# A fused long-convolution and MLP block on one core: the front's small rows turned on TensorE, two swap buffers exchanged, the half block of w3 on two column groups, and some sixty moves in a written order

## The chip, the cores and the metric

The kernel runs on one core of a Trainium2 chip. The time is that of one execution on the device, in microseconds (us). Engines: PE is TensorE (matrix multiplication), DVE VectorE, ACT ScalarE, POOL GpSimd, SP the engine whose queue issues most DMAs. PEld is PE's loading of weights, which overlaps its matmuls.

## The reference, cut to what matters

S = 2048 tokens, D = 640 channels, hidden width F = 1728, all in bf16.

```python
mod = silu(c) @ w_mod                      # six vectors: sa, ca, ga, sb, cb, gb
x = A_q
h = layernorm(x) * (1 + ca) + sa           # q of block A
k_shift[s] = sum over t<4 of k[s-t] * shift_k[:, t]
kv = k_shift * v
y = irfft(rfft(kv, 4096) * rfft(ssm_k, 4096))[:2048] + kv * ssm_D
x = x + ga * (h * y)
h = layernorm(x) * (1 + cb) + sb           # input of block B
g = gelu(layernorm(h) @ w1)                # its four channel quarters are shifted by 1, -1, 2, -2 tokens
x1 = h + shifted(g) @ w2
h2 = gelu(layernorm(x1) @ w3) @ w4         # w3: 640 x 1728, w4: 1728 x 640
return x + gb * (x1 + h2)
```

## The kernel before

The whole kernel is one list of tasks. `add(engine, cost, f, r=, w=)` of a `Planner` records a task: a function that emits instructions for one engine, and the keys (a buffer and a range of it) that it reads and writes. From the keys follow the dependences and thus the semaphores. The costs in `add` set nothing here: a string `ORDER`, written out in the source, gives the order in which the tasks are emitted and the engine of each (`88P:0` is task 88 on PE with PSUM place 0; S is SP, D DVE, A ACT, G POOL). Each engine runs its own tasks strictly in that order, and SP's order is the order of its DMAs. A task that waits holds back all that stands behind it on its engine.

Big buffers in SBUF are used again and again by range: `Ra`, `Rb`, `RG`, `RH`, `RK`, `RQ`, `R3`, `R5`, `T01`.

**Front (0 to about 20 us).** The long convolution is a Fourier transform of length 4096 in two stages of small matrix products. Its sine and cosine tables are made on the chip: POOL's iota gives integers, DVE scales them and masks them (`angles`, L292 and L293) or POOL does it in turns (`angles_pool`, L306 to L310), and ACT takes the sine (`sin_to` L321, `turns_to` L316). `F1bd` is the table of stage 1, `Gs` that of stage 2 (its third part is the negative of its first, L348). The per-partition constants for this (`pidx`, `pci`, `s32`, `s64`, `offc`) are 15 tiny DVE operations, L263 to L279. Meanwhile SP loads, in this order: D (L224, into `Dcol`, one column per block of 128 channels), four blocks of ssm_k (L228), shift_k (L229, into `skT`), the fifth block, then k and v by transposing DMAs (L233, `kT` and `vT`), and much later c (`c_col`, at 38.8 us). D and c come as 640 separate elements of 2 bytes, shift_k as 640 pieces of 8 bytes. D is added to the first tap of ssm_k (L444, three times on POOL, twice on DVE), and a block is turned in 32x32 squares by DVE (`to_slots`, L394).

**Transforms (8 to 95 us).** Stage 1 (L407) multiplies the turned blocks, first of ssm_k, then of kv, by `F1bd` into PSUM; ACT and DVE copy the result to `T01` (L207 is that copy on ACT, L209 on DVE). Stage 2 (L427) uses two row groups of 64 rows side by side. The shifts of k are matmuls with diagonal matrices (L463; `diagw`, made by POOL from `skT`, L355), and DVE multiplies by v (L468). The spectra are then multiplied (L617, DVE; 20 products). For these the upper and the lower halves of the partitions have to be swapped by pairs of DMAs (L613, one by SP, one by POOL) into a ring of four buffers:

```python
KSY = [(RG[:, 6144:8192], ...), (RK[:, 0:2048], ...), (RK[:, 2048:4096], ...), (Rb[:, 8192:10240], ...)]
```

The inverse goes through L628 and L629 and then, per group of token tiles, through 32x32 products (`inverse2`, L661).

**Modulation.** silu(c) is computed on POOL; PE multiplies it with w_mod, loaded in ten pieces (`mod_half`, L487, L493), and ACT writes the vectors (L497 to L508).

**Token tiles (56 to 299 us).** 16 tiles of 128 tokens go through `make_q` (first layer norm, L601, L602), `chain_a` (times q, L737, added to x, L740), `chain_b` (second layer norm, L755, L756), `chain_c` (third one, into the mixer). Layer norms take a sum from DVE, a sum of squares from ACT (`square_sum`, L729), a few tiny operations on POOL or DVE (`ln_finish`, L702 to L717), and a normalisation on DVE (L594) or ACT (L592). The normalised tile is turned by five PE matmuls (L772) and copied by ACT (L778) or DVE (L780), or it is turned by SP's transposing DMA (L765). Then PE does w1 (L818, L828), w2 (L873; DVE adds, L880), and, in groups of one or two tiles with all tokens of a group side by side, w3 (`mm_w3`, L907) and w4 (`mm_w4`, L937). There are nine such groups: seven of two tiles, and two of one tile (the first and the last).

F = 1728 is 13 blocks of 128 and a **half block** of 64. Before, the half block of w3 is filled up to 128 columns with a second copy of its 64 columns (POOL, L1020), so that its matmuls are of the same shape as all others, and its result stands twice, on partitions 0 to 63 and 64 to 127. In w4 the half block multiplies 64 rows only: `half`, L928, takes tile 0 from the lower 64 partitions and tile 1 from the upper ones, on two row groups. ACT's gelu (L911) takes up to four blocks at a time, and the last piece holds blocks 12 and 13. DVE adds the rest (L960, L965, L966) and SP stores the tile in four DMAs (L969; for the last tile L981, L984, L987).

The main loops of `mm_w3` before:

```python
for fl in range(fn):
    fb = f0 + fl
    for b in range(ND):
        nc.tensor.matmul(pt[:, fl, 0:cw], lhsT=w3_sb[:, b, fb * P:(fb + 1) * P], rhs=xT[:, b, 0:cw],
                         start=(b == 0), stop=(b == ND - 1))
```

## Time and profile before

| | |
|---|---|
| time, median of 3 runs | 302.58 us (300.95 to 302.81) |
| span of the profiled execution | 298.7 us |
| what lies around the span, from span to median | 3.9 us |
| PE, DVE, ACT, POOL busy | 269.7, 218.2, 208.3, 104.8 us |
| mean granted clock of PE | 0.975 |
| first transpose, first matmul | 6.01, 8.12 us |
| PE busy of 40 us, 100 to 140 us | 29.6 us |
| last matmul starts | 293.69 us |

The profiled execution is known by its span alone, so its own time is taken as the span and the 3.9 us around it. The profile is that of one execution. Its rows give, for a group of instructions, the line of the source, the engine, the operation, out<-in with the shape, the count, the busy time and mean duration of one, and the idle time of the engine ahead of them with what ended it. Rows of the timeline give start and duration in us. Rows of the table by stage give the stretch and its length, the busy time and number of instructions of PE, PEld, DVE, ACT and POOL, the granted clock of PE (1 is full), the share of time for which the 16 DMA engines are busy, and GB/s. Matmuls are pipelined, and their ends are modelled, so a matmul's price is better read from the distance between starts.

### The profile page before, as it was taken

Reading aid. Unit: us, or ns where it says so; the run is one execution under the profiler, and the core shown is the slowest. Engines: PE = TensorE matmul, PEld = TensorE weight load, DVE = VectorE, ACT = ScalarE, POOL = GpSimd, SP = SyncE. Lnnn points to the kernel's source line nnn. Section 1 sums busy time; section 2 is a strip of 40 time slices with the busy share of each in tenths; the row PEclk is TensorE's granted clock in tenths of the full one; section 3 lists DMA queues with packets and bytes.
Section 4 is the critical chain, followed back from the end, with each engine's and each line's share of the span. In section 5 each row is a group of like instructions: output and inputs, shape, how many; then the busy total and the mean of one; then the engine's idle time right before and its main releaser. Section 6 shows DMA issues by size and latency. Waiting matters only on the chain.

```text
span 298.7 us, 7890 instructions
## 1 busy us (share of the span) xinstructions
PE 269.7 (90%) x3176; PEld 208.5 (70%) x3182; DVE 218.2 (73%) x438; ACT 208.3 (70%) x341; POOL 104.8 (35%) x237
## 2 busy tenths in 40 slices
PE   0999999999989766869999999999999999999993
PEld 0666755777878436648878677787788767887871
DVE  8998999999999998898759589886361544212442
ACT  4799989999999789979868775766854705431200
POOL 5864364453216591434275426120421321100000
PEclk9999999999999859799999999999999999999999
DMA  6999999898999920563700203223113030510112
GB/s 215 275 215 184 225 137 246 225 217 221 229 253 281 280 65 2 153 203 69 273 4 0 46 5 68 56 46 60 41 40 80 5 89 6 63 43 23 29 52 60
DMA packets 58356, 35.76 MB, mean 120 GB/s; under 512 B 40032, under 2 KB 55008, under 8 KB 58320
## 3 DMA queue, kind: packets, MB, share of 16 engines
q1 hardware_dynamic: 57136, 32.01, 46.3%
q0 software_dynamic: 1088, 3.21, 4.1%
q8 instruction: 25, 0.41, 0.6%
q14 instruction: 11, 0.09, 0.1%
q10 hardware_dynamic: 96, 0.04, 0.1%
HBM read 16.31 MB, written 2.62 MB: 63 GB/s over the span
## 4 chain that ended last, share of the span: by engine, by line
PE 51%; DVE 13%; ACT 11%; DMA 10%; POOL 6%; issue 5%; SPq 2%; DVEq 0%; POOLq 0%; ACTq 0%
PE ps_w L937 17%; PE ps_w L907 14%; ACT T L207 5%; DMA Ra<-in_A_q_dram 5%; PE ps_w L873 4%; PE ps_w L818 3%; PE ps_s L427 3%; ACT RG L729 3%; DVE Rb L617 3%; PE ps_ksh L463 2%; POOL lnv L715 2%; PE ps_s L407 2%; DMA RK<-R 2%; DVE R L756 2%; PE ps_mod L493 2%
## 5 line engine op out<-in xcount | busy, mean ns | idle before, releaser
L907 PE MATMUL ps_w<-R,T 128*128 128x256 bf16 (+1 forms) x630 | 63.8, 261 | 0.7 <-DMA R<-RH 0.7
L907 PEld LDWEIGHTS <-T 128*128 128x128 bf16 x630 | 55.5, 98 | 7.9 <-issue 2.0
L937 PE MATMUL ps_w<-T,R 128*128 128x320 bf16 x416 | 59.1, 299 | 0.0
L911 ACT ACTIVATE R<-ps_w 128x1024 bf16<-128x1024 f32 (+2 forms) x36 | 28.8, 827 | 41.9 <-PE ps_w L907 41.9
L937 PEld LDWEIGHTS <-R 128*128 128x128 bf16 x416 | 40.5, 98 | 15.2
L960 DVE TENSOR_TENSOR T<-ps_w,R 128x640 bf16<-128x640 f32 x15 | 12.3, 822 | 35.4 <-PE ps_w L928 18.1
L207 ACT CAST T<-ps_s 128x1024 bf16<-128x1024 f32 x32 | 30.4, 1029 | 3.2 <-PE ps_s L407 3.1
L207 ACT CAST R<-ps_s 128x960 bf16<-128x960 f32 (+1 forms) x35 | 30.8, 964 | 1.8 <-PE ps_s L427 1.6
L407 PE MATMUL ps_s<-F1bd,Rb 128*128 128x256 bf16 x160 | 23.3, 298 | 8.7 <-DVE Rb L394 8.1
L729 ACT ACTIVATE RG<-R 128x640 bf16<-128x640 bf16 x32 | 23.5, 734 | 9.9 <-DVE R L880 6.7
L407 PEld LDWEIGHTS <-Rb 128*128 128x128 bf16 x160 | 16.7, 107 | 14.7 <-DVE Rb L394 8.6
L873 PE MATMUL ps_w<-RG,R 128*128 128x320 bf16 x160 | 23.2, 299 | 2.1 <-ACT R L820 2.1
L715 POOL TENSOR_TENSOR lnv<-lnv,mhalf 128x2 f32<-128x2 f32 (+1 forms) x29 | 22.5, 775 | 2.3
L427 PE MATMUL ps_s<-T,RG 64*128 64x160 bf16 x512 | 21.2, 230 | 0.8 <-ACT R L207 0.6
L880 DVE SCALAR_TENSOR_TENSOR R<-ps_w,R 128x640 bf16<-128x640 f32 x16 | 12.9, 819 | 11.8 <-PE ps_w L873 11.6
L427 PEld LDWEIGHTS <-RG 64*128 64x128 bf16 x512 | 17.7, 94 | 5.1 <-issue 4.6
L818 PE MATMUL ps_w<-R,RG 128*128 128x256 bf16 (+1 forms) x200 | 20.0, 259 | 1.3 <-DMA R<-RK 0.6
L873 PEld LDWEIGHTS <-R 128*128 128x128 bf16 x160 | 15.4, 98 | 8.2 <-ACT R L820 2.4
L629 PE MATMUL ps_i<-EB,Rb 128*128 128x128 bf16 x160 | 19.0, 219 | 1.5 <-DVE Rb L617 1.4
L818 PEld LDWEIGHTS <-RG 128*128 128x128 bf16 x200 | 17.1, 102 | 3.5 <-issue 2.0
L628 PE MATMUL ps_i<-EA,Rb 128*128 128x128 bf16 x160 | 19.0, 219 | 0.4 <-ACT R L207 0.3
L714 POOL TENSOR_TENSOR lnv<-stat,lnv 128x2 f32<-128x2 f32 x19 | 4.0, 212 | 40.9 <-ACT RG L729 28.7
(178 smaller groups left out, 513.5 us busy)
## 6 DMA issues: line engine op xcount, KB each, us to landing
Ra<-in_A_ssm_k_dram SPq DMA_DIRECT2D x5, 512.0 KB, 5.7
R<-in_w_mod_dram SPq DMA_DIRECT2D x6, 400.0 KB, 6.0
out_dram<-RH SPq DMA_DIRECT2D x60, 40.0 KB, 1.6
T<-in_B_w_dram SPq DMA_DIRECT2D x5, 432.0 KB, 6.2
RH<-in_w_mod_dram SPq DMA_DIRECT2D x4, 400.0 KB, 4.4
Ra<-in_A_q_dram SPq DMA_DIRECT2D x4, 320.0 KB, 6.6
RK<-R SPq DMA_DIRECT2D x5, 256.0 KB, 4.5
RK<-R POOLq DMA_DIRECT2D x5, 256.0 KB, 5.3
```

The costliest lines, as they stand in the source:

```text
L207: nc.scalar.copy(dst, src(ps.tile))
L407: nc.tensor.matmul(psv[:, ml, :], lhsT=xL[:, s0:s0 + P], rhs=F1r, start=True, stop=True)
L427: nc.tensor.matmul(psv[:, g, j], lhsT=Gs[p, k, 64 - 64 * cc:192 - 64 * cc], rhs=T1h[h][p, cc * 32 + k], start=(cc == 0), stop=(cc == 1), t ...
L628: nc.tensor.matmul(psv[:, w, :], lhsT=Av[:, r_, :, g_], rhs=EAf, start=True, stop=False)
L629: nc.tensor.matmul(psv[:, w, :], lhsT=Bv[:, r_, :, g_], rhs=EBf, start=False, stop=True)
L715: nc.gpsimd.tensor_tensor(rs, rs, mhalf[:, 0:n], ALU.pow)
L729: add("ACT", 0.74, lambda e: nc.scalar.activation(junk, src, ACT.Square, scale=float(D) ** -0.5, accum_out=stat[:, li, 1, t:t + 1]), r=[sk ...
L818: nc.tensor.matmul(pt[:, fb, 0:cw], lhsT=w1_sb[:, b, 160 * fb:160 * fb + P], rhs=hT[:, b, 0:cw], start=(b == 0), stop=(b == ND - 1))
L873: nc.tensor.matmul(pt[:, hf, 0:320], lhsT=gsf[:, fb, c0:c0 + P], rhs=w2_sb[:, fb, 320 * hf:320 * hf + 320], start=(fb == 0), stop=(fb == 4))
L907: nc.tensor.matmul(pt[:, fl, 0:cw], lhsT=w3_sb[:, b, fb * P:(fb + 1) * P], rhs=xT[:, b, 0:cw], start=(b == 0), stop=(b == ND - 1))
L911: nc.scalar.activation(g3[g % 2][:, f0:f0 + fn, 0:cw], ps.tile[:, 0:fn, 0:cw], ACT.Gelu_apprx_tanh)
L937: nc.tensor.matmul(bank(i, hf), lhsT=gg[:, fb, i * P:(i + 1) * P], rhs=w4_sb[:, fb, 320 * hf:320 * hf + 320], start=(fb == 0 and i == 0), ...
```

## The change

It has four parts.

1. **Front.** D, shift_k and c are loaded as five contiguous rows each (128, 512 and 128 elements a row) into a free corner of `T01`; D first of all, the other two after three blocks of ssm_k. PE turns them with matmuls of five columns against a 5x5 identity (`eye`, made on POOL), one ahead of its first stage-1 matmul and five after two stage-1 tasks; ACT copies the result from PSUM (`Dcol`; `csk`, which holds c and shift_k). c is no longer loaded at 38.8 us. Of the tiny constants, DVE keeps 9 operations and POOL takes 6. The two 512-wide scale steps of the first table go from DVE to ACT (Identity), the negated table goes from DVE to ACT, two additions of D go from POOL to DVE. ACT's first instruction is a sine of one column.
2. **Swap buffers.** The third and fourth buffers of `KSY` are exchanged. The DMAs that write them change places on SP and POOL.
3. **Half block.** The copy that filled w3 up is gone. Its 64 columns are multiplied on two column groups: tile 0 into the lower 64 partitions, tile 1 into the upper 64 (in a group of one tile, that tile into both). So there are ten matmuls of 128 columns in place of five of 256 (or five of 128). Gelu's last piece is 384 columns wide in place of 512.
4. **Order.** Behind the front, some sixty tasks change place or engine. On PE the moves are by one to five places. From DVE to ACT go one evacuation of stage 1 (at 55 us) and six normalisations; from ACT to DVE three normalisations, two copies of turned tiles, one evacuation of the inverse and one of the modulation; from POOL to DVE three small statistics steps, and one back. On SP, a half load of w4 goes ahead of loads of w3, and stores of output tiles change order. PE has 233 tasks where it had 231, ACT 254 for 248, DVE 304 for 301, POOL 94 for 97, SP 169 as before.

The diff, without the string `ORDER`:

```diff
-    KSY = [(RG[:, 6144:8192], ("RG", 6144, 8192)), (RK[:, 0:2048], ("RK", 0, 2048)), (RK[:, 2048:4096], ("RK", 2048, 4096)), (Rb[:, 8192:10240], ("Rb", 8192, 10240))]
+    KSY = [(RG[:, 6144:8192], ("RG", 6144, 8192)), (RK[:, 0:2048], ("RK", 0, 2048)), (Rb[:, 8192:10240], ("Rb", 8192, 10240)), (RK[:, 2048:4096], ("RK", 2048, 4096))]
...
-    dma("SP", 8, lambda q: ld_tiny(q, Dcol[:], A_ssm_D.rearrange("(b p) -> p b", p=P)), w=[("Dcol", 0, 1)], rate=8.0)
+    dma("SP", 8, lambda q: q.dma_start(rowD, A_ssm_D.rearrange("(b p) -> b p", p=P)), w=[("T01", 0, P)])
...
-    dma("SP", 8, lambda q: q.dma_start(skT[:], A_shift_k.rearrange("(b p) j -> p b j", p=P)), w=[("skT", 0, 1)], rate=30.0)
-    dma("SP", 8, lambda q: ld_tiny(q, c_col[:], c.rearrange("o (b p) -> p (o b)", p=P)), w=[("ccol", 0, 1)], rate=12.0)
+    dma("SP", 8, lambda q: q.dma_start(rows, A_shift_k.rearrange("(b p) j -> b (p j)", p=P)), w=[("T01", 2 * P, 6 * P)])
+    dma("SP", 8, lambda q: q.dma_start(rowc, c.rearrange("o (b p) -> (o b) p", p=P)), w=[("T01", P, 2 * P)])
...
+    add("POOL", 0.2, lambda e: nc.gpsimd.affine_select(out=eye, in_=one.to_broadcast([P, ND]), ...
+    def f(e):
+        pt = pst(psD, name="ps_row")
+        nc.tensor.matmul(pt[:, 0, 0:ND], lhsT=rowD, rhs=eye[0:ND, :], start=True, stop=True)
+    add("ACT", 0.1, lambda e: nc.scalar.activation(lnv[:, 2, 0:1], b_pos[:], ACT.Sin), ...
+    t1 = add("ACT", 0.2, lambda e: nc.scalar.copy(Dcol[:], psD.tile[:, 0, 0:ND]), ...
...
+        nc.tensor.matmul(pt[:, 0, 0:ND], lhsT=rowc, rhs=eye[0:ND, :], start=True, stop=True)
+        for j in range(4):
+            nc.tensor.matmul(pt[:, 0, ND + ND * j:2 * ND + ND * j], lhsT=rows.rearrange("b (p j) -> b j p", j=4)[:, j, :], rhs=eye[0:ND, :], start=True, stop=True)
...
+            if split:
+                add("ACT", 0.25 + 0.00095 * n, lambda e, m_=m_, off=off: nc.scalar.activation(m_, ti, ACT.Identity, scale=s_col, bias=off),
+                    r=[keys[0], ("scol", 0, 1)], w=[k_])
...
+            if e == "ACT":
+                nc.scalar.mul(Gs[:, k2s, 128:192], Gs[:, k2s, 0:64], -1.0)
...
+                    if fb == NF - 1:
+                        for b in range(ND):
+                            for i in range(2):
+                                c0 = P * i if cw > P else 0
+                                nc.tensor.matmul(pt[64 * i:64 * i + 64, fl, 0:P], lhsT=w3_sb[:, b, fb * P:fb * P + 64], rhs=xT[:, b, c0:c0 + P],
+                                                 start=(b == 0), stop=(b == ND - 1), tile_position=(0, 64 * i))
+                        continue
...
+                if cw > P and f0 + fn == NF:
+                    n = cw * (fn - 1) + P
+                    gf = g3[g % 2].rearrange("p f n -> p (f n)")
+                    nc.scalar.activation(gf[:, f0 * cw:f0 * cw + n], ps.tile[:].rearrange("p f n -> p (f n)")[:, 0:n], ACT.Gelu_apprx_tanh)
...
-            nc.tensor.matmul(bank(i, hf), lhsT=gg[p, NF - 1, i * P:(i + 1) * P], rhs=w4_sb[p, NF - 1, 320 * hf:320 * hf + 320],
+            nc.tensor.matmul(bank(i, hf), lhsT=gg[p, NF - 1, 0:P], rhs=w4_sb[p, NF - 1, 320 * hf:320 * hf + 320],
...
-        nc.gpsimd.tensor_copy(w3_sb[:, :, F:FP], w3_sb[:, :, F - 64:F])
-    add("POOL", 0.6, f, w=[("T01", 0, ND * FP)])
```

## The prediction

> **What bounds the kernel now.** I read the summary rows first, then the busy time by stage, then single stretches.
>
> ```profile
> PE 269.7 (90%) x3176; PEld 208.5 (70%) x3182; DVE 218.2 (73%) x438; ACT 208.3 (70%) x341; POOL 104.8 (35%) x237
> ...
> PE   0999999999989766869999999999999999999993
> ...
> DVE  8998999999999998898759589886361544212442
> ACT  4799989999999789979868775766854705431200
> ...
> PEclk9999999999999859799999999999999999999999
> ```
>
> PE is busy for 90%, but not evenly: one empty slice at the start, a hollow at slices 13 to 18, and the last slice. The table by stage (PE, PEld, DVE, ACT, POOL, granted clock, DMA share, GB/s) says who fills each stage:
>
> ```profile
> 0.00:8.00 8.00, 0.00 (x0) 0.00 (x0) 6.84 (x31) 3.15 (x5) 4.68 (x15) 1.00 0.67 230
> 8.00:20.00 12.00, 11.83 (x65) 7.92 (x67) 11.93 (x12) 10.25 (x12) 10.25 (x8) 1.00 1.08 247
> ...
> 40.00:50.00 10.00, 9.95 (x85) 6.00 (x85) 9.62 (x12) 8.86 (x11) 7.11 (x10) 1.00 1.03 172
> ...
> 80.00:95.00 15.00, 13.48 (x219) 12.38 (x219) 15.00 (x17) 14.97 (x20) 4.88 (x5) 1.00 1.00 252
> ...
> 105.00:110.00 5.00, 2.83 (x99) 1.30 (x96) 4.77 (x15) 4.48 (x12) 4.71 (x8) 0.50 0.33 78
> ...
> 150.00:170.00 20.00, 20.00 (x177) 16.15 (x174) 14.19 (x36) 14.63 (x28) 11.60 (x31) 1.00 0.09 18
> ...
> 215.00:286.00 71.00, 71.00 (x631) 55.90 (x629) 25.61 (x55) 28.01 (x48) 9.78 (x32) 1.00 0.22 42
> ```
>
> So: 0 to 8 us waits for the first data; 8 to 95 us fills DVE above all (PE and ACT nearly), while the DMA share is about 1; 100 to 140 us is a chain of short dependent steps, with PE 29.6 of 40 us busy; from 140 us on PE alone counts, with 2.2 us idle up to 286 us. In the first stage only the front's start matters, in the last only PE work.
>
> **Part 1, the front.** The start in the timeline:
>
> ```profile
> 5.54 0.44 POOL L444 TENSOR_TENSOR Ra<-Ra,Dcol 128x1 bf16<-128x1 bf16 x1 [1.82 <-DMA Ra<-in_A_ssm_k_dram]
> ...
> 6.01 3.96 DVE L394 STREAM_TRANSPOSE Rb<-Ra 128x1024 int32<-128x1024 int32 x2
> ...
> 8.12 1.25 PE L407 MATMUL ps_s<-F1bd,Rb 128*128 128x256 bf16 x5 [8.12 <-DVE Rb L394]
> ```
>
> The first ssm_k load is issued at 1.32 and lands at 5.40 us, 4.1 us, beside the 640 two-byte pieces of D (issued 0.80, landed 3.75). A 440 KB load on idle queues at 122.2 us took 3.3; so I estimate 3.5 for 512 KB without the pieces: landed at 4.8. The add (L444) goes from POOL (0.44) to DVE (0.17). DVE is free for it: before the transpose it loses two L292 of 0.54 and some 0.5 of tiny operations, while it ended its tables at 5.93. The transpose starts near 5.0 instead of 6.0: **−1.0**. Until 18 us DVE also loses the negated table (L348, 0.74 at 9.9 us), and gains a second add (0.16): −0.6 more, as transposes follow each other there. ACT takes two table steps (some 0.65 each, in the 2.1 and 1.3 us that it waits for L293), the negation (0.65) and two copies of 0.2 each.
>
> New is a wait: PE's turning of D before the first matmul, and of c and shift_k (five matmuls of five columns) after two stage-1 groups. Behind the second stand PE's stage 1 and, through the shared buffer T01, ACT's evacuations; its rows are issued after three ssm_k loads. Below: nothing, as PE waits for transposes there anyway. Above: rows landing with the next load, 9.4 us, against PE being ready at some 8.5, so 0.9. I take 0.2.
>
> Then it must survive to 95 us. The vT transposing load that landed at 39.19 feeds L468 at 39.28; only the 0.8 us or so by which the queue runs earlier help it. The c load (issued 38.83, landed 43.82: 5.0 us for 1.3 KB) leaves the queue before the loads landing at 45.73 and 50.38, so those come 2.5 us earlier (5.0 less the usual 2.4 pitch). The evacuation moved from DVE to ACT at 55 us (1.19) and the small one back (0.43) give DVE 0.8, but ACT has only 1.1 us idle at 40 to 50. Of 1.4 at 18 us plus 0.8 of DVE work I let 1.5 arrive: **−1.5** (0.8 if the 39 us load pins it, 2.4 if all arrives).
>
> **Part 2, the swap buffers.** Before, the swap into RK's upper half is issued at 70.97, since its buffer is busy until then, lands at 76.59, and the product (L617) reads it at 76.67; the swap into Rb is issued at 59.59, lands at 68.18 and is wanted at 78.95. Exchanged, the early buffer serves the early product. DVE is idle only 0.2 in 67 to 80 us, so this alone is worth at most 0.2: **−0.1**. Without it the 76.6 us landing would swallow part 1.
>
> **Part 3, the half block.** Rows of the groups:
>
> ```profile
> L907 PE MATMUL ps_w<-R,T 128*128 128x256 bf16 x490 | 55.7, 273 | 0.7 <-DMA R<-RH 0.7
> ...
> L907 PE MATMUL ps_w<-R,T 128*128 128x128 bf16 x140 | 8.5, 219 | 0.0
> ```
>
> 70 matmuls are one group, so there are 7 groups of two tiles and 2 of one. Ends are modelled, so I price by distance: 30 of N=256 took 3.27 us, 109 ns each; N=128 stand 56 ns apart. Each of the 7 groups swaps 5×109 = 0.55 for ten of N=128 in five pairs; each of the 2 swaps 5×56 = 0.28 for the same ten. If a pair runs side by side it costs 58: 0.29. Two rows speak for that: L427's pairs on two row groups start 4 ns apart, and L661's 32x32 tiles follow at 7 to 10 ns with 160 columns each, which four row groups alone could not do (L427's pair with 160 columns takes 69, so four would give 17 each).
>
> Against it stands a rule: the Trainium skill, "TensorEngine Tiling (Array Packing)", Key Properties, says a change of tiling mode drains TensorE. The trace has such a change:
>
> ```profile
> 271.12 0.57 PE L937 MATMUL ps_w<-T,R 128*128 128x320 bf16 x3
> 271.62 0.45 PE L928 MATMUL ps_w<-T,R 64*128 64x320 bf16 x4
> 272.00 0.50 PE L907 MATMUL ps_w<-R,T 128*128 128x256 bf16 x3
> ```
>
> Three L937 of 136 ns are 0.41, yet L928 starts 0.50 later: 0.09 on entering. Two pairs of 0.14 are 0.28, yet L907 comes 0.38 later: 0.09 on leaving. So the rule holds, and costs 0.18 a group. By the naive rows the part gives 7×(0.55−0.29) = −1.8; with the drain 7×(0.55−0.47) − 2×(0.47−0.28) = **−0.2**. I take −0.2. The other end: that page (Restrictions) has column tiling switch off Fast Weight Load; no run here shows the effect. If pairs then took turns, a group costs 0.56+0.18 = 0.74: 7×0.19 + 2×0.46 = +2.3. The range of this part is −1.8 to +2.3.
>
> L911's last piece shrinks from 512 to 384 columns, some 0.15 of ACT, hidden (L911 waits 41.9 us for PE). The POOL copy (L1020, 0.45 at 135.5) goes. Only L907 waits for it, and that starts at 135.74, just when PE's work before it ends (ten L873 from 134.38 at 0.136): nothing is held, so nothing is won. If earlier parts bring PE there sooner, the copy, queued behind POOL's L717 until 135.45, would have held it; without it that gain passes.
>
> **Part 4, the moves.** After 140 us, moves of norms between ACT (0.91) and DVE (0.44) cost nothing: both idle over a quarter of the time. They can only fill PE's 2.2 us: among these a step from L873 to L907 of 0.95 (DMA R<-RH, 0.7) and one from L928 to L818 of 0.89 (DMA R<-RK, 0.6), both behind DMA transposes whose norms the change touches. In 100 to 140 us the gap is 10.4 us, held by POOL's small layer-norm steps (L714, L715: 0.2 + 0.7 apiece), ACT's squares (0.74) and DVE. There DVE takes two turns (L780, 0.49 each, for ACT's 0.68), an evacuation (1.15 for 0.96) and a small statistics step of POOL's (some 0.3), and gives one norm at 124 us (0.45, on ACT 0.91): DVE gets 2.0 more, ACT 1.4 less. With DVE and ACT at 89 and 90% this can go either way: −1.5 to +1.2. SP's half load of w4 goes ahead of w3's loads: 80 KB, some 0.3 us at the DMA rates of the table, where w3's last load landed at 132.98 and L907 starts at 135.74: hidden. Reordered output stores are off the path except the last (SP, 294.6). I take one of the two PE gaps (0.8 over a normal step), 0.4 in the hollow and 0.2 at the end: **−1.4**, range −3.7 (both gaps, 1.5 in the hollow, 0.7 at the end) to +1.2.
>
> **Sum.** The execution's span is 298.7, and 3.9 lie around it to the median of 302.58 (300.95 to 302.81); I keep these. −1.5 −0.1 −0.2 −1.4 = −3.2 (the turning wait is within the −1.5): **299.4**. The measurement can tell about 1%, 3.0 us, from no change, so 299.55 is the border.
>
> **Rivals.**
> *The hollow closes* (20%). If the earlier data and moves keep PE from the 0.50 granted at 105 to 110 us, its 2.83 us busy there halve, 0.70 and 0.68 elsewhere rise too, and 1.5 + 0.7 more go: −5.4, 297.2. For: a chain of short steps reacts to order. Against: its links are POOL, ACT and DVE, not PE.
> *The front stops at the loads* (20%). L468 at 39.3 us and full DMA (share 1.0 to 1.17) hold the gain at 0.8, and moves give 0.4: −1.5, 301.1. For: three loads land within 0.1 to 0.65 us of their use.
> *Column groups don't run side by side* (12%), which is also the case that part 3 doesn't do what it says: +2.3 instead of −0.2, and, as it sits in the PE-bound stage, nothing hides it. With the front's 0.8 and 0.4 of the moves alone, 302.6 − 1.2 − 0.1 + 2.3 = 303.6, slower than before. It decides from a group of 0.72 us (7×0.17 + 2×0.44 = 2.1) if the rest gives under 2; with the moves at +1.2 it passes 305.6.
> *The forecast* (48%): 298.2 to 300.6.
>
> Faster by over 1%: 20% and two thirds of the 48, 0.52. Slower by over 1%: the last rival's upper half, and moves gone wrong, 0.09. Within 1%: 0.39. The range takes 296.3 (hollow and both gaps) to 302.6 (the loads pin, pairs half exposed).
>
> **What would show it.** First transpose at 5.0 us, first stage-1 matmul at 7.1; the product that read RK at 76.67 without a wait and near 75; PE's steady stretch beginning some 2 us before 140; L907's last five steps at 0.47 for both kinds of group; PE gaps at 170 and 205 us gone. Wrong: a first matmul after 7.8, L468 still waiting for a load near 39, pairs over 100 ns apart, or the hollow's length unchanged while DVE is longer in it.

## The result, and the profile after

| | before | after |
|---|---|---|
| time, median of 22 executions each, same chip | 302.27 us (300.66 to 304.39) | 300.87 us (299.70 to 304.87) |
| ratio after to before | | 0.9955, 95% interval 0.9936 to 0.9973 |
| span of the profiled execution | 298.7 us | 299.9 us |
| span of a second profile of each | 300.0 us | 298.9 us |

The change gains 1.4 us (0.8 to 1.9), less than half of the 3.2 that were forecast. The profiled spans alone would say the opposite. Each time is its own span and 1.7 us (301.59 and 299.9 after, 301.78 and 300.0 in the second execution of before); so the profiled execution of before was some 2 us faster than the median, and the 3.9 us that the forecast carried "around the span" were 1.7 and a lucky execution. The two profiled executions of before lie 1.2 us below its median on the mean, those of after 0.2 above. Below, stages are therefore compared over several profiles, and what a whole kernel wins is told by the medians alone.

The summary rows of after (busy time, share and count; then the 40 slices of 7.5 us, in tenths):

```profile
PE 270.9 (90%) x3227; PEld 206.8 (69%) x3233; DVE 217.8 (73%) x437; ACT 211.8 (71%) x347; POOL 105.8 (35%) x235
...
PE   0999989999889668689899999999999999999993
...
DVE  7998989899999989998748888877460444221443
ACT  7999979999999698998788975775954713432200
...
PEclk9999999999999855999999999999999999999998
```

The shape is the same: a start, a hollow at slices 12 to 18, a steady stretch. PE has 51 matmuls more (six for the turned rows, 45 for the half blocks). The table by stage (PE, PEld, DVE, ACT, POOL, granted clock, DMA share, GB/s):

```profile
0.00:8.00 8.00, 1.17 (x6) 0.83 (x7) 6.22 (x25) 5.32 (x10) 6.68 (x20) 1.00 0.71 258
8.00:20.00 12.00, 11.38 (x74) 7.11 (x73) 11.77 (x11) 11.39 (x14) 9.35 (x8) 1.00 1.05 231
40.00:50.00 10.00, 9.28 (x81) 5.76 (x81) 8.76 (x11) 7.80 (x10) 6.21 (x9) 1.00 1.16 211
80.00:95.00 15.00, 13.39 (x218) 12.26 (x215) 15.00 (x14) 14.95 (x20) 3.50 (x5) 1.00 0.94 231
105.00:110.00 5.00, 3.13 (x85) 1.62 (x84) 4.46 (x12) 5.00 (x13) 3.40 (x7) 0.50 0.67 143
150.00:170.00 20.00, 20.00 (x181) 16.22 (x180) 14.55 (x41) 16.81 (x31) 9.14 (x24) 1.00 0.07 11
215.00:286.00 71.00, 71.00 (x640) 54.96 (x639) 25.31 (x56) 27.87 (x48) 10.22 (x32) 1.00 0.22 45
```

PE has 1.17 us of work ahead of 8 us, where it had none: the front starts earlier. But from 40 to 50 us PE does 9.28 where it did 9.95, and DVE 8.76 for 9.62: something takes time there, though no engine is busier. The start, in the timeline (start, duration):

```profile
4.68 0.16 DVE L478 TENSOR_TENSOR Ra<-Ra,Dcol 128x1 bf16<-128x1 bf16 x1 [0.43 <-DMA Ra<-in_A_ssm_k_dram]
4.88 2.08 DVE L428 STREAM_TRANSPOSE Rb<-Ra 128x1024 int32<-128x1024 int32 x1
...
7.01 1.89 PE L441 MATMUL ps_s<-F1bd,Rb 128*128 128x256 bf16 x8 [4.64 <-DVE Ra L478]
```

The transpose starts at 4.88 and the first matmul at 7.01, for 6.01 and 8.12 before. The stages by milestones, in us; the last column is a kernel of the experiments, the changed one with 64 idle matmuls at the start:

| | before, two profiles | after, two profiles | after, 64 idle matmuls |
|---|---|---|---|
| first transpose | 6.01, 6.01 | 4.88, 4.95 | 4.87 |
| fifth transpose | 16.46, 16.64 | 15.36, 15.33 | 15.32 |
| last product of shifted k with v | 52.33, 53.12 | 53.04, 53.16 | 52.30 |
| eleventh spectral product | 82.35, 83.13 | 83.72, 83.50 | 82.64 |
| first w3 | 135.74, 136.81 | 137.24, 135.90 | 135.35 |
| from there to the last half block of w4 | 157.95, 158.25 | 157.69, 158.03 | 156.51 |

The lead of 1.1 to 1.3 us at 16 us is gone at 53 us, and turned into a loss of some 0.9 at 83. From the first w3 on, 0.2 us are won. At the last half block the two kernels' profiles are level (294.38 and 294.43 on the mean): the 1.4 us of the medians are about the luck of the profiled executions of before, so where they arise is read from the stages that differ in all profiles.

### The profile page after: what moved, and what is told of

It is laid out like the page before. It is cut to its first block, busy times and chain, and to the rows that moved or that the text cites. A ratio compares the mean times of both kernels' runs of the same rounds, so it can differ in the third digit from the quotient of the medians.

```text
span 299.9 us, 8004 instructions
## 1 busy us (share of the span) xinstructions
PE 270.9 (90%) x3227; PEld 206.8 (69%) x3233; DVE 217.8 (73%) x437; ACT 211.8 (71%) x347; POOL 105.8 (35%) x235
## 4 chain that ended last, share of the span: by engine, by line
PE 67%; ACT 18%; DVE 6%; DMA 3%; issue 3%; POOL 1%; SPq 1%; ACTq 0%; DVEq 0%; POOLq 0%
PE ps_w L982 19%; PE ps_w L947 18%; ACT T L208 9%; PE ps_w L906 6%; PE ps_ksh L497 5%; PE ps_s L461 4%; PE ps_w L851 4%; PE ps_s L441 4%; ACT R L208 3%; DMA T<-in_B_w_dram 2%; ACT RG L762 2%; PE ps_mod L527 2%; DVE R L210 1%; PE ps_w L973 1%; DMA Ra<-in_A_ssm_k_dram 1%
## 5 line engine op out<-in xcount | busy, mean ns | idle before, releaser
L947 PE MATMUL ps_w<-R,T 128*128 128x256 bf16 (+1 forms) x585 | 61.0, 261 | 0.6 <-DVE R L813 0.6
L947 PEld LDWEIGHTS <-T 128*128 128x128 bf16 x585 | 51.0, 98 | 8.0 <-issue 1.8
L956 ACT ACTIVATE R<-ps_w 128x1024 bf16<-128x1024 f32 (+2 forms) x29 | 25.1, 885 | 28.2 <-PE ps_w L947 28.1
L208 ACT CAST T<-ps_s 128x1024 bf16<-128x1024 f32 x33 | 31.5, 1033 | 3.5 <-PE ps_s L441 3.4
L441 PE MATMUL ps_s<-F1bd,Rb 128*128 128x256 bf16 x160 | 22.8, 286 | 6.1 <-DVE Ra L478 4.6
L441 PEld LDWEIGHTS <-Rb 128*128 128x128 bf16 x160 | 15.8, 102 | 12.0 <-DVE Ra L478 4.7
L748 POOL TENSOR_TENSOR lnv<-lnv,mhalf 128x2 f32<-128x2 f32 (+1 forms) x29 | 23.1, 797 | 2.3
L461 PE MATMUL ps_s<-T,RG 64*128 64x160 bf16 x512 | 21.4, 230 | 1.0 <-ACT R L208 0.8
L461 PEld LDWEIGHTS <-RG 64*128 64x128 bf16 x512 | 17.9, 94 | 5.5 <-issue 4.8
L851 PE MATMUL ps_w<-R,RG 128*128 128x256 bf16 (+1 forms) x200 | 20.0, 258 | 0.6 <-ACT R L867 0.6
L497 PE MATMUL ps_ksh<-R,RQ 128*128 128x512 bf16 x74 | 18.2, 380 | 1.1 <-ACT R L208 0.9
L851 PEld LDWEIGHTS <-RG 128*128 128x128 bf16 x200 | 17.0, 101 | 2.8 <-issue 1.3
```

The costliest lines, as they stand in the source:

```text
L208: nc.scalar.copy(dst, src(ps.tile))
L441: nc.tensor.matmul(psv[:, ml, :], lhsT=xL[:, s0:s0 + P], rhs=F1r, start=True, stop=True)
L461: nc.tensor.matmul(psv[:, g, j], lhsT=Gs[p, k, 64 - 64 * cc:192 - 64 * cc], rhs=T1h[h][p, cc * 32 + k], start=(cc == 0), stop=(cc == 1), t ...
L497: nc.tensor.matmul(pt[:, i, :], lhsT=diagw[:, b, jj, :], rhs=kT[:, b, c0:c0 + 512], start=(jj == 0), stop=(jj == 3))
L748: nc.gpsimd.tensor_tensor(rs, rs, mhalf[:, 0:n], ALU.pow)
L851: nc.tensor.matmul(pt[:, fb, 0:cw], lhsT=w1_sb[:, b, 160 * fb:160 * fb + P], rhs=hT[:, b, 0:cw], start=(b == 0), stop=(b == ND - 1))
```

## The experiments

The changed kernel's lines are some 30 to 45 higher than those of before: L441 is the stage-1 matmul (L407 before), L461 stage 2, L497 the shifts of k, L502 their product with v, L650 the spectral product, L947 and L943 are w3 and its half block, L861 and L851 are w1, L634 is the second step of a first layer norm.

### 1. Front and order apart

`before_again` and `after_again` are the two kernels once more, for second profiles. `late_undone` is the changed kernel with the old order behind its first 62 us, `late_only` the kernel before in its first 62 us, with the new order behind them:

```diff
 late_undone:
-ORDER: the changed kernel's
+ORDER: the changed kernel's up to 62 us, then that of before (tasks renumbered); swap buffers and half block stay changed
 late_only:
-ORDER: that of before
+ORDER: that of before up to 62 us, then the changed kernel's (tasks renumbered)
-    KSY = [..., (RK[:, 2048:4096], ...), (Rb[:, 8192:10240], ...)]
+    KSY = [..., (Rb[:, 8192:10240], ...), (RK[:, 2048:4096], ...)]
```

> The kernel before unchanged, for a second profiled execution. Theory 1: PE reaches the same place of the instruction stream near 39.8 us, some 0.4 us or less after its instructions have come, so without a pause or a short one; two pauses of 1.8 and 2.1 us in the stretch from 100 to 109 us, again at block boundaries of the instruction stream. Rival (accidents): the pauses stand elsewhere or are gone. Span 298 to 301 us.

> The changed kernel unchanged, for a second profiled execution. Theory 1 (the front's lead of 1.0 us is taken back where PE waits for its own instructions): again a lead of about 1.0 us at 30 us, and again a PE pause of 0.5 to 1.0 us near 38 us, at the same place of the instruction stream, though the semaphore that the instruction waits for was there by 37.0. Rival (an accident of one execution): no pause there, and a lead of 1 us that lasts to 60 us; span 1 us shorter than 299.9. Time by both: 0.995 of before.

> The changed kernel's first 62 us (front, and the few moves among them), its exchanged swap buffers and its half block, with the order of before behind 62 us. Theory A (the late moves bring what was measured, about 1.5 us, by closing the two PE gaps of 0.7 us near 170 and 205 us, and the front brings nothing): the time of before, 1.000 (0.998 to 1.003), with the two gaps back. Theory B (the front brings it, the late moves nothing): 0.995, that of the changed kernel. Both half: 0.9975.

> The kernel before for its first 62 us, with its front and its half block as they were; behind 62 us the order of the changed kernel, with the exchanged swap buffers. Theory A (the moves behind 62 us bring what was measured): 0.994 to 0.997 of before, PE gaps near 171 and 207 us (0.5 and 0.55 to 0.85) gone. Theory B (only front and moves together do it): 0.999 to 1.003.

Measured: `after_again` 0.9937 (0.9909 to 0.9965), `late_undone` 0.9994 (0.9964 to 1.0024), `late_only` 0.9970 (0.9947 to 0.9993). The front, the swap buffers and the half block together give nothing that can be measured; the new order with the exchanged swap buffers, without front and half block, gives 0.3%. `late_only` goes from its first w3 to the last half block in 156.50 us, 1.45 and 1.75 less than the two profiles of before. Before has two PE gaps in this stage, at 170 and 206 us (what waited, for what, total us, times, longest):

```profile
PE ps_w L907 <- DMA R<-RH: 0.7, 1, 0.7
PE ps_w L818 <- DMA R<-RK: 0.6, 1, 0.6
```

Both are gone in `late_only`, and in all kernels with the new order: under 0.1 us is left there, in `old_half` 0.37. In `late_undone` the first is back with 0.60 us; of the second, 0.22.

### 2. Where the front's lead goes: the instruction stream

PE's part of the timeline of after, 36 to 47 us (in brackets the idle time ahead, and its releaser):

```profile
36.77 1.00 PE L461 MATMUL ps_s<-T,RG 64*128 64x160 bf16 x24
38.69 1.90 PE L497 MATMUL ps_ksh<-R,RQ 128*128 128x512 bf16 x8 [0.91 <-ACT R L208]
40.52 0.86 PE L461 MATMUL ps_s<-T,RG 64*128 64x160 bf16 x20
```

PE stands for 0.91 us ahead of L497. The row names ACT, but the ACT instruction whose semaphore is waited for had ended at 37.0. What is late is another thing, which two rows show (queue and kind, packets, MB, share of 16 engines), the first from the page, the second from the stretch 36.2 to 36.5 us:

```profile
q8 instruction: 25, 0.41, 0.6%
```

```profile
q8 instruction: 1, 0.02, 19.7%
```

25 packets of 16 KB for 6460 instructions of PE: one for 256 instructions. PE's pauses without an open semaphore fall on the same place of every 256 recorded instructions, and end 2.3 to 2.8 us after such a packet starts (36.26 to 38.68; in other stretches and kernels 36.7 to 39.12, 98.84 to 101.45, 105.68 to 108.20). By the count, PE enters the block before at some 30.5 to 32.5 us in these kernels. Where few loads run, the next packet starts 0.2 to 1.2 us after such an entry (in after at 111.7 and 117.1 us). Here the token loads, issued from 26.7 to 29.2, and the transposing loads fill the DMA engines, and it starts only at 35.8 to 37.0. No record shows the request itself, so that it waits behind these loads is read from the times. In the kernel before PE needs the packet at 39.81 and it is there at about 39.4 (37.0 and the usual 2.4); its second profile shows no pause (a row without brackets has no idle time ahead):

```profile
37.96 1.00 PE L427 MATMUL ps_s<-T,RG 64*128 64x160 bf16 x24
38.89 1.90 PE L463 MATMUL ps_ksh<-R,RQ 128*128 128x512 bf16 x8
```

PE runs 1 us earlier now, and waits for it: 0.91, and 0.72, 0.38, 0.37 and 1.22 in `after_again`, `late_undone`, `old_half` and `swap_back`. Two further waits for evacuations, 0.27 at 42.6 and 0.39 at 48.9, take the rest.

If so, the lead must come back when the limits of these blocks of 256 instructions are moved. PE idles from 2.4 to 7 us, so idle matmuls there cost nothing and shift every limit behind:

```diff
         pt = pst(psD, name="ps_row")
         nc.tensor.matmul(pt[:, 0, 0:ND], lhsT=rowD, rhs=eye[0:ND, :], start=True, stop=True)
+        pad = psA.tile([P, 2, 512], F32, name="ps_pad", tag="q3")
+        for _ in range(64):     # 96 and 80 in two others; each is 2 instructions of PE
+            nc.tensor.matmul(pad[:, 0, 0:ND], lhsT=rowD, rhs=eye[0:ND, :], start=True, stop=True)
```

> The changed kernel with 64 idle matmuls of five columns added ahead of PE's first work, into a PSUM place that is free: 128 more instructions, in a time (2 to 7 us) in which PE has nothing to do. They move the boundaries of PE's instruction blocks 128 instructions forward. Theory 1 (PE pauses because the 256-instruction block that it needs is fetched late, and arrives some 2.4 us after its DMA packet, which the token loads delay to 36 us): the boundary now falls near 33.5 us, so PE pauses there until about 38.5, 4 to 5 us long, and the time is 2 to 4 us longer. Rival (the pause near 38 us comes from something else in the kernel, and not from the instruction stream): the pause stays at the same matmul near 38 us, time unchanged.

> The same with 96 idle matmuls, 192 instructions. Theory 1: the boundary before it now falls near 25.5 us, ahead of the token loads (issued from 26.7), so the next block is fetched by 29 us and there is no pause at 32 or 38 us; PE's lead at 42 us is 0.4 to 0.9 larger than in the changed kernel. In time 0 to 1 us, as the later boundaries, in the stretch of 32x32 products, move too. Rival (no effect of the instruction stream): pause at 38 us, time unchanged.

> The kernel with 64 idle matmuls again, since its time (0.990) went against theory 1 as I had put it, and its one profiled execution was late from 12 us on by a collision (a one-column addition on DVE took 2.50 us beside a 2.47 us operation on POOL). Theory 1 amended (what counts is where the block boundaries fall against the loads, in the front and again from 95 to 110 us): 0.988 to 0.993 again, and a profile without the collision shows PE pauses without a semaphore of less than 2 us in all up to 110 us, where the changed kernel has 2.4 to 4. Rival (the 0.990 was chance): 0.994 to 0.997.

> 80 idle matmuls. Theory 1: the second boundary falls at 26 us, just ahead of the token loads, so no pause at 33 or 38 us, PE's lead over before at 53 us 0.7 or more; from 95 to 110 us boundaries near 98.7 and 104, pauses unknown, 1 to 4 us. Time 0.990 to 1.003. Rival (time does not depend on the boundaries): as the changed kernel, 0.994 to 0.996.

Measured: 64 matmuls 0.9902 (0.9870 to 0.9933) and again 0.9900 (0.9870 to 0.9931), 80 matmuls 0.9903 (0.9870 to 0.9937), 96 matmuls **1.0035** (1.0005 to 1.0065): 298.7, 299.0 and 303.2 us. The same work, on a path where PE is idle, makes 1.3% by its number. So the time does depend on where the limits fall. Where they fall well was not foreseen: 64 was to be 2 to 4 us slower and 96 up to 1 us faster, and both went the other way; 0.988 to 0.993, said after that for 64 again, was met, and 80 is where the stream theory had it, outside its rival's 0.994 to 0.996. With 64 the pause at 38 us is gone:

```profile
37.01 1.00 PE L464 MATMUL ps_s<-T,RG 64*128 64x160 bf16 x24
37.95 1.90 PE L500 MATMUL ps_ksh<-R,RQ 128*128 128x512 bf16 x8
39.78 0.87 PE L464 MATMUL ps_s<-T,RG 64*128 64x160 bf16 x20
```

Its packet starts at 26.1 to 28.4 us in the three kernels (64 in its second profile), ahead of the rush. With 96 a limit falls badly in the hollow, next to the loads of the modulation and the weights, and PE stands for 4.03 us:

```profile
99.36 0.82 PE L697 MATMUL ps_i<-T,RH 32*32 32x160 bf16 x58
104.20 0.32 PE L697 MATMUL ps_i<-T,RH 32*32 32x160 bf16 x6 [4.03 <-issue]
```

The packet of that stall starts at 101.54 us, 2.66 ahead of the resumption; the first w3 comes at 138.25, 2.9 later than with 64.

The profiled execution of the first 64-matmul kernel had lost its lead for another reason; see the last section.

### 3. What the padding buys

Idle matmuls again, 70, 70 and 64, so that the limits lie as in the changed kernel with 64, in the kernel before (reading zero columns of `kT`), in `late_only` and in `late_undone`:

```diff
+                    for _ in range(70):     # 64 in late_undone, at D's turning as above
+                        nc.tensor.matmul(pad[0:16, 0, 0:ND], lhsT=kT[0:ND, 0, 0:16], rhs=kT[0:ND, 1, 0:ND], start=True, stop=True)
                 psv = pst(ps, name="ps_s1")
```

> The kernel before with 70 idle matmuls of five columns ahead of PE's first work (140 instructions, so that its instruction blocks begin at the same matmuls as in the changed kernel with 64). Theory F (the boundaries matter because they take back the front's lead): before has no pause at 38 us to lose, so 0.997 to 1.002. Theory P (the boundaries are worth 1% by themselves, through the stretch from 95 to 140 us, whatever the front): 0.990 to 0.994.

> The old front and the new order behind 62 us, with the swap buffers exchanged, and the same 70 idle matmuls. Theory F: as without them, 0.995 to 0.998, so that the front is worth 0.5% of the 0.990 once its lead is not taken back. Theory P: 0.989 to 0.992, the front nothing.

> The new front, swap and half block with the order of before behind 62 us, and 64 idle matmuls: the front's worth by itself, with its boundary ahead of the token loads. Theory F: the lead of 0.8 us stays to 93 us and reaches the end, 0.995 to 0.998 (0.9994 without the padding). Rival (the old order gives the lead back between 95 and 140 us): 0.998 to 1.001 in spite of a lead at 93 us.

Measured: `before_pad` 0.9979 (0.9955 to 1.0003), `late_only_pad` 0.9916 (0.9892 to 0.9940), `late_undone_pad` 1.0008 (0.9979 to 1.0037). This was not what a front freed of its pause should give: the padding pays with the new order, front or no front, and not measurably with the old one. With the limits alike, the new order and its swap buffers are worth 0.6% or 1.9 us (`late_only_pad` against `before_pad`, whose intervals lie apart). With the old order the padding too shortens the stage behind the first w3 (157.43 us in both kernels, for 157.95 to 158.94 without it), but the hollow, from the last spectral product to the first w3, is longer in these profiles (44.04 and 44.31, for 43.17 to 43.47 in three of the four without; 44.12 in `half_only`). Beside the full kernel's 0.990, the new front is worth 0.16% or 0.5 us, which the intervals don't separate; in the profiles its lead of 1.1 us at the eleventh product (83.73 and 82.64) is 0.6 at the last half block of w4 (292.46 and 291.86).

### 4. The wait at 142 us

The changed kernel has a gap of its own. After the first w3, in the second profile of after (first what waited, for what, total us, times, longest; then PE's timeline):

```profile
PEld L861 <- DMA R<-RK: 1.7, 1, 1.7
...
PE ps_w1x L861 <- DMA R<-RK: 1.6, 1, 1.6
```

```profile
137.79 2.41 PE L947 MATMUL ps_w<-R,T 128*128 128x128 bf16 x40
140.10 0.90 PE L805 MATMUL ps_tr<-RG,RH 128*128 128x128 bf16 x10
142.58 0.72 PE L861 MATMUL ps_w1x<-R,RG 128*128 128x256 bf16 x5 [1.57 <-DMA R<-RK]
```

L861 takes a normalised tile turned by SP's transposing DMAs, two of them, issued at 136.63 and 138.00. The first lands after 2.65 us. The second has moved all but seven of its 640 packets by 140.14, but PE goes on at 142.58. At 140.38 an instruction packet of PE starts. The two go together in every profile with the new order. The gap is there in the five in which a packet starts 2.0 to 2.4 us after the second load's issue (at 139.3 to 141.5 us), and ends 2.1 to 2.3 after the packet's start: 1.22 us in after, 1.57 in `after_again`, 1.24 in `swap_back`, 1.51 in `old_half`, 1.19 in `x_light`. Where the packet comes ahead of that issue, or over 6 us behind it, the reader goes on as soon as 2.6 us after the issue, with no gap or one of 0.3 (`late_only`, `late_only_pad`, `pad_64`, `pad_64_again`, `pad_80`, `pad_96`, `swap_back_pad`). To test it, 64 idle matmuls went into stretches behind 124 us in which PE waits anyway, 32 and 32, so that only the later limits move; and as the converse these same 64 went into the kernel that has 64 at the start, which puts the later limits back (256 instructions more):

```diff
+    def idle(what, at, place):
+        calls[what] += 1
+        if calls[what] == at + 1:
+            pad = psA.tile([P, 2, 512], F32, name="ps_pad", tag="q" + place)
+            for _ in range(32):
+                nc.tensor.matmul(pad[:, 0, 0:ND], lhsT=ident[0:ND, :], rhs=ident[0:ND, 0:ND], start=True, stop=True)
...
+            idle("tr", 3, ps.place)      # ahead of the fourth tile turned by PE, 125 us
             pt = pst(ps, [P, 2, 8, P], BF, name="ps_tr")
...
+                idle("w2", 1, "2")       # ahead of the second w2, 131 us
                 pt = pst(ps, name="ps_w2")
```

> The changed kernel with 64 idle matmuls of five columns, 32 each in two stretches in which TensorE waits anyway (about 124.7 and 130.8 us in its second profile). Everything before 124 us is the changed kernel's, the pause at 38 us among it; behind 132 us TensorE's instruction stream lies as in the kernel with 64 idle matmuls at the start. Theory L (what padding wins, it wins behind 124 us: the 16 KB instruction packet that starts at 139.3 to 141.5 us, just behind the second of the two transposing loads of RK, goes with a wait of 1.2 to 1.6 us before L861; moved, the wait is gone): packet near 137, no TensorE gap over 0.3 us between 140 and 145 us, ratio 0.990 to 0.992. Rival E (padding wins in the front and the hollow, the late gap is a coincidence): the gap at 142 stays or another takes its place, ratio 0.994 to 0.996.

> 64 idle matmuls at the start and the same 64 in the late stretches: the stream behind 132 us lies as in the changed kernel again (256 instructions more), the front and the hollow as in the kernel with 64 at the start. Theory L: an instruction packet at about 139 to 141 us, a TensorE gap of 1.2 to 1.6 us near 141 again, ratio 0.994 to 0.996. Rival E: no gap, ratio 0.989 to 0.991 as with the front's 64 alone.

Measured: `pad_late` 0.9934 (0.9908 to 0.9960), `pad_both` 0.9945 (0.9916 to 0.9974). The traces do what theory L says. In `pad_late` the packet starts at 137.70 and there is no gap; from the first w3 to the last half block it takes 156.49 us. In `pad_both` the packet starts at 139.12, and the gap is back, between two rows that were one stretch with 64 alone:

```profile
139.42 0.91 PE L818 MATMUL ps_tr<-RG,RH 128*128 128x128 bf16 x10
141.52 0.72 PE L874 MATMUL ps_w1x<-R,RG 128*128 128x256 bf16 x5 [1.20 <-ACT RG L583]
```

It takes 157.65 us there, and 156.51 with the front's 64 alone. So the gap is worth 1.1 to 1.5 us, and the packet's place makes it. That rests on the traces. The medians go along for `pad_both`, 299.85 us against 298.69 (0.9945 for 0.9900), but the two are separate runs and their intervals overlap (0.9916 to 0.9974, 0.9870 to 0.9931). For `pad_late` they don't settle it: 0.9934 lies between what L (0.990 to 0.992) and E (0.994 to 0.996) said, and its interval overlaps that of after. What the padding wins in the full kernel is then in the main the late gap, 1.1 to 1.5 us; `late_only` has no such gap, and what its padding won was 1.1 us ahead of the first w3 (137.05 and 135.97 in one profile each), for which no cause was shown.

In this gap PE does not lack instructions: it is the load that is late. In `after_again` the last seven of its packets of 256 bytes start only at 141.24 to 141.44 us, when the instruction packet (140.38 to 141.25) has ended. The six profiles of the new order with the gap, `pad_both` among them (its packet starts 1.8 us after the issue), show 3 to 13 such stragglers each; no other profile shows any. The load counts its semaphore up in 16 steps. The last comes 4.15 to 4.53 us after the issue in these six, and 2.59 to 2.61 in thirteen others; PE goes on 0.04 to 0.05 us after it in the six. The order is not needed for this: `late_undone`, with the old order, has its packet at 140.38, 2.16 us after the issue, no straggler, but the last step late, and PE waits 0.70 us (start, us and what of its chain there):

```profile
138.22 4.18 DMA R<-RK
142.40 0.14 issue
```

Why the last step still comes about 1 us after the last straggler, or late without one, is not shown.

### 5. The hollow's loads

From 95 to 140 us, PE pauses for instruction blocks in nearly all profiles near 101 and 108 us (0.4 to 2.8 us, 4.0 in `pad_96`), and is granted half its clock for 10.2 to 17.1 us. To see whether DMA traffic sets the length of the hollow, this kernel leaves out six of the eight token tiles 8 to 15 of the load of x:

```diff
-    def x_load(a0, a1, r=()):
+    def x_load(a0, a1, r=(), ae=None):
...
-    x_load(8, 12, y0)
-    x_load(12, NT, y0)
+    x_load(8, 12, y0, 9)      # a0, a1, wait, end of what is loaded
+    x_load(12, NT, y0, 13)
```

> The changed kernel, with the loads of token tiles 8 to 15 cut to two tiles of the eight (0.96 MB of the 3.4 MB that are loaded between 93 and 108 us left out, so the result of the other six tiles is not that of the reference). Theory 1 (the loads delay the instruction fetch, and that makes PE pause at 101 and 108 us and its clock fall to one half): fetches start under 1 us after a boundary near 105 us, the second pause (0.6 to 1.5 us) goes, half clock ends one or two steps of 3.4 us earlier, 1.5 to 4 us faster than the changed kernel: 0.982 to 0.991. Rival (the stretch is set by the chain of DVE, ACT and POOL): within 0.5 us of the changed kernel.

Measured: 0.9950 (0.9921 to 0.9978), as after, and not the 0.982 to 0.991 of theory 1. The second pause is gone and the half clock down to 10.2 us (`pad_both` has 10.2 too, with all its loads), and the time stays. Neither sets the time here: PE's pauses there lie beside the chain of DVE, ACT and POOL, unless one is as long as 4 us.

### 6. Half block and swap buffers

`old_half` is the changed kernel with the full last block of w3 and POOL's copy; `half_only` the kernel before with the new half block. `swap_back` has the old order of `KSY` and of its DMAs in the changed kernel, `swap_back_pad` the same with 64 idle matmuls at the start:

```diff
 half_only (old_half undoes the same):
+                    if fb == NF - 1:
+                        for b in range(ND):
+                            for i in range(2):
+                                c0 = P * i if cw > P else 0
+                                nc.tensor.matmul(pt[64 * i:64 * i + 64, fl, 0:P], ..., tile_position=(0, 64 * i))
+                        continue
-        nc.gpsimd.tensor_copy(w3_sb[:, :, F:FP], w3_sb[:, :, F - 64:F])
 swap_back, swap_back_pad:
-    KSY = [..., (Rb[:, 8192:10240], ...), (RK[:, 2048:4096], ...)]
+    KSY = [..., (RK[:, 2048:4096], ...), (Rb[:, 8192:10240], ...)]
```

> The changed kernel with the old half block: w3 filled up to 14 whole blocks by the copy on POOL, five matmuls a group, gelu over 512 columns. Theory by the drain (0.09 us on entering and on leaving the column mode, read from the profile of the changed kernel: a group costs 0.50 against 0.55 of old pairs and 0.28 of old singles): -7x0.05 + 2x0.22, so +0.1 or less between the two: ratio of this kernel to before as that of the changed kernel, within 0.001. Rival (without a drain, 0.29 a group): this kernel 1.8 us slower than the changed one, about 1.001 of before.

> The kernel before with the new half block alone (ten matmuls on two column groups, gelu of 384 columns, no copy on POOL). By the drain (a group of 0.50 against 0.55 and 0.28 us): +0.1 us, 0.999 to 1.001. Rival (the 0.3% by which the kernel with the old half block was behind the changed one is the half block's own): 0.996 to 0.998.

> The changed kernel with the third and fourth swap buffer, and their DMAs, as before. My step 2 (the landing at 76.6 us would swallow the front's lead): since the front has no lead left at 68 us, the pin no longer binds and the time is that of the changed kernel within 0.2 us, 0.994 to 0.996; DVE waits some 0.1 to 0.5 before the sixth product. Rival (the late swap holds the products of the new order): 0.5 us or more slower, 0.997 or more.

> The changed kernel with 64 idle matmuls and the old swap buffers. By my step 2 (the late swap of the old buffers swallows a lead of the front): the lead of 0.8 us at 68 us is gone at the sixth product, 0.993 to 0.995 against 0.990. Rival (its swap comes earlier too with the earlier start): 0.989 to 0.992.

Measured: `half_only` 0.9997 (0.9971 to 1.0022): the half block does nothing to the time that can be seen. `old_half` 0.9976 (0.9949 to 1.0003), 0.2% above after where 0.1% at most was expected, but not resolved from it; its profiled execution had a step of half clock more, 3.4 us at 142.7 us, behind its gap of 1.51. In the timeline of after a group looks so:

```profile
279.01 1.83 PE L947 MATMUL ps_w<-R,T 128*128 128x128 bf16 x25
280.76 0.47 PE L943 MATMUL ps_w<-R,T 128*64 128x128 bf16 x10
281.16 1.29 PE L947 MATMUL ps_w<-R,T 128*128 128x128 bf16 x20
```

By the single instructions, the two matmuls of a pair start 3 to 4 ns apart and the pairs 56 ns; entering takes 203 ns for the usual 109, leaving 151 for 56. A group costs 0.40 from its start to the next L947, and 0.09 on entering: 0.50.

`swap_back` 0.9995 (0.9963 to 1.0026), `swap_back_pad` 0.9903 (0.9866 to 0.9940). The first looks as if the exchange were worth 1.3 us; with the padding nothing of it can be seen in the time. Both times lie where the rival had them, not where the wait's theory did. The trace shows the wait that was forecast: without the exchange the sixth product starts at 78.12 us, for 76.84 with it (both with the padding), and the lead is swallowed. But at the last half block 0.7 us of this is left (292.59 and 291.86, one profile each).

## Why the prediction was right or wrong

**Part 1, the front: the start right, the survival wrong.** 4.88 and 7.01 us, for 5.0 and 7.1; the lead at 16 us 1.1 to 1.3, for 1.4 at 18. The step that failed is "Of 1.4 at 18 us plus 0.8 of DVE work I let 1.5 arrive": at 53 us nothing arrives. The load that was feared, at 39 us, does not hold it: the product behind it starts at 38.7 and 38.6. PE's own instructions do (0.91 us at 38.7, 0.72 in the second profile), which were no resource in the sum. At the end, the medians leave the front, swap buffers and half block together 0 to 0.5 us of the 1.5: 0.9994 in `late_undone`, and 0.990 for 0.9916 with the padding, which is not resolved. Where the pause is taken away, some 0.6 us arrives by the profiles; the hollow takes the rest of the 1.1 (42.49 us, for 42.02 in `late_only_pad`).

**Part 2, the swap buffers: the wait as forecast, its worth not resolved.** −0.1 was forecast, and with the padding 0.9903 and 0.990 stand beside each other, each some 0.3% uncertain. "Without it the 76.6 us landing would swallow part 1" is what the trace shows, for the product; at the last half block 0.7 us was left, in one profile each. In after the sixth product starts at 77.56 and 77.67, not "near 75": the lead was already gone.

**Part 3, the half block: right.** Sum with the measured group: 7×(0.50 − 0.55) + 2×(0.50 − 0.28) = +0.1, for −0.2 forecast. The pairs run side by side. The rule of the Trainium skill ("TensorEngine Tiling (Array Packing)", Key Properties) that a change of tiling mode drains the array decided it: 94 ns in and 95 out for column groups, where the row groups had shown 0.09 each. Without the rule and the rows for its price the forecast would have been −1.8. Whether the fast weight load is lost, as that page's Restrictions say of column tiling, these times don't tell: loading 64 columns takes 110 ns, 128 columns 98, and the pairs' pitch of 56 ns shows no cost of it.

**Part 4, the moves: right behind 140 us, and given back.** Forecast was one of two PE gaps, 0.8, and 0.2 at the end. Both went, and without the gap at L861 this stage is 1.45 and 1.75 us shorter (156.5 for 157.95 and 158.25). That gap gives 1.2 to 1.6 back. It was not in the range's working: of a step that moves, its place in the instruction stream was not asked. With the limits alike the order and its swap buffers are worth 1.9 us, for the 1.4 of this part. The other term, 0.4 won in the hollow, is there: from the last product to the first w3 it takes 42.0 to 43.3 us in thirteen profiles with the new order (45.47 in `pad_96`, with its stall) and 43.2 to 44.3 in the six with the old. But ahead of it the same order loses some 0.4 by a move that the sum did not price at its new place. A half norm now stands among the spectral products, where DVE has no idle time. DVE's timeline of `late_undone` (old order), then of `after_again`:

```profile
73.13 0.48 DVE L634 TENSOR_TENSOR RQ<-RQ,modv 128x640 bf16<-128x640 bf16 x1
73.54 1.22 DVE L210 CAST T<-ps_i 128x1024 bf16<-128x1024 f32 x1
```

```profile
73.07 0.89 DVE L634 TENSOR_TENSOR RQ<-RQ,modv 128x640 bf16<-128x640 bf16 x2
73.87 1.22 DVE L210 CAST T<-ps_i 128x1024 bf16<-128x1024 f32 x1
```

Two in place of one, and the next step 0.80 after them for 0.41: from the first to the eleventh product it takes 14.25 us for 13.79 (13.90 and 13.91 before). In single profiles the hollow brings it back or not: 43.17 and 43.47 before, 43.30 and 42.18 after.

**The sum.** Against the profiles of before, after stands at +0.9 at the eleventh product (0.4 of it the moved norm, the rest the pause and its two followers beside a lead that is spent), +0.3 at the first w3 and 0.05 at the last half block: the hollow gives 0.6 back, the late stage 0.2. The forecast had −1.6 for the front and −1.4 for the moves by then. The medians, which hold 22 executions of each, say −1.4; between this and the profiles lies the spread of single executions, 1.1 us in the hollow of after alone. Two slips of the working did not move the number: PE's idle time from 140 to 286 us is 1.6 us by the rows of the table by stage, not 2.2, and the last rival with the moves at +1.2 comes to 305.2, not over 305.6.

**The rivals.** "The front stops at the loads" has the number (301.1; measured 300.9), not the mechanism: the loads hold up the instruction packet, not the data. The hollow did not close: it is some 1 us shorter with the new order, and its half clock is still there. The column groups do run side by side.

**Best version.** The changed kernel with 64 or 80 idle matmuls: 298.7 (64 in its second run) and 299.0 us, 1.0% below before and 0.5% below the change.

## What to carry to other kernels

An instruction stream of thousands of short matmuls is itself a load: where the rest of the program fills the DMA queues, PE may stand for its next block, and the profile then names a semaphore that was satisfied long ago, or "issue". The block's packet can also hold up a load that runs beside it, and so the data that PE waits for. So before a change of 0.5% is believed or dropped, shift the stream by some idle instructions in a place where the engine waits, and time it again: here that made 0.990 or 1.0035 of one and the same kernel. And a lead early in the program is worth only what the engine that sets the next stage lets through: measure it at milestones, in more than one profile.

## What was unexpected of the hardware

- One packet of 16 KB for 256 instructions of PE, usable 2.3 to 2.8 us after it starts; late by up to some 6 us, by the count, where loads fill the DMA engines; pauses of 0.3 to 4.0 us.
- A transposing DMA of 640 packets with such a packet 1.8 to 2.4 us after its issue: complete 4.15 to 4.53 us after the issue, for 2.6 in the other profiles. In six of these seven its last 3 to 13 packets of 256 bytes started only after the instruction packet had ended.
- Half clock was granted in steps: 10.2, 13.7 or 17.1 us in the hollow, 3.4 us apart, in both kernels, and the number changed between executions of one kernel.
- An addition of one column on DVE, 0.16 us elsewhere, took 2.50 while POOL ran an operation of 2.47. This is the profiled execution of the first 64-matmul kernel, and it cost its front 2.5 us:

```profile
9.69 2.50 DVE L481 TENSOR_TENSOR Ra<-Ra,Dcol 128x1 bf16<-128x1 bf16 x1 [0.59 <-DMA Ra<-in_A_ssm_k_dram]
9.70 2.47 POOL L392 TENSOR_SCALAR_AFFINE_SELECT RQ<-csk 128x2560 bf16<-128x2560 bf16 x1
```

- Executions of one kernel on one chip spread over 3 to 5 us (300.66 to 304.39 before), more than this change is worth.
